# Back transform, join and first MLP steps of a long-convolution and MLP kernel: reordered hand-over between two stages

## The chip, the cores and the metric

The kernel runs on one core of a Trainium2 chip. The metric is the device time of one launch in microseconds; lower is better. A core has TensorE (PE in the rows, with PEld for its weight loads), VectorE (DVE), ScalarE (ACT), GpSimd (POOL) and SyncE (SP), which here only issues DMAs. ScalarE issues DMAs too.

## The reference

A long convolution by FFT, gated by its input, and then an MLP on all tokens (B = 2, S = 12480, D = 128, d_ff = 2048):

```python
h_filt = (np.maximum(pos_emb @ w1, 0.0) @ w2) * np.exp(-0.01 * pos)[:, None]
u = x * v
y = irfft(rfft(u, 2*S) * rfft(h_filt, 2*S), 2*S)[:, :S, :]   # along the sequence
a = (x * y).reshape(B * S, D)
h = a @ w_in
return np.maximum(0.01 * h, h) @ w_out
```

## The kernel before

The transform of length 98 x 128 is split into 98-point and 128-point parts that are matmuls with constant matrices. The program has three stretches:

- **First forward part of batch 0 and of the filter** (up to about 180 us of the span), bound by DMA.
- **The head's second stretch** (about 180 to 350 us), the loop `for i, c in enumerate(ORD)` over 25 chunks of four columns (`KC = 4`): forward 128-point transform (`fwd`), product with the filter's spectrum (`product`, multiplications and one addition on VectorE, the subtraction on GpSimd except in the last two rounds), back transform (`back_halves`, one round late), evacuation from PSUM (`evac`, both copies on ScalarE), store to the DRAM scratch `scr2`. The order ORD ends with chunks 10 and 11. The last two chunks also go straight from SBUF into the first tile's input `cin[0]` (`last_c`, eight small DMAs in all), so that the first tile need not wait for the scratch. Beside that, `weights()` (the generator `wprep`) splits the float64 MLP weights into two float32r parts; its last two operations make `wc_h` (ScalarE) and `wc_l` (VectorE).
- **The MLP** over 50 blocks of at most 512 tokens (block 0 has 390), each of 16 steps: `m1(k, f)` is three matmuls into `mh` (w_in_h by zh, w_in_h by zl, w_in_l by zh), ScalarE and VectorE make the two parts rh and rl of the activation, and three steps later `m2` adds three matmuls into `acc`.

A **tile t** is one pair of the 64 output pairs per batch. Its input `cin` is read from `scr2` (`upper_c`: five DMAs of the upper rows; `rows_c`: two of the lower rows), and `gt`, `xm` by `load_gx`. `join_hi` (two additions) and `join_lo` (six: two into `cq`, four into `cp`) put the halves together; `front` runs the last transform (16 matmul records into `yp`), multiplies by x (`zt`), transposes (`zp`), copies to `zf` (three ScalarE copies) and splits into zh (ScalarE) and zl. For tile 0 joins run on VectorE, for tiles 1 and 2 on GpSimd; tiles 0 and 1 share the one buffer of `cp`.

**Batch 1** is convolved by the generator `conv1`, whose pieces are spread between other work. Its first part has 16 groups of two halves; a half has four pieces: a pause, then eight matmuls and a ScalarE copy of the second PSUM tile, then VectorE's addition, then VectorE's subtraction (`add_sub`). The function `late()` stores the group before (two DMAs). `ahead(n)` runs n halves. Six halves and one piece (`AHEAD = 25`) run before the MLP's loop: two before the chunk loop, two between the loop and the last back transform, one after it, and one inside the first tile's front. The rest is paced from step 14 of the MLP on, so that the first part is done at step 120 whatever AHEAD is. `mult_a(c)` is GpSimd's product x*v for group c.

Each engine takes its instructions in program order (`manual_schedule`); GpSimd, having little before it, runs far ahead. SyncE takes nearly all loads and stores in program order and waits in order, so a load that waits for a store holds what stands behind it. Steps such as `turn_at`, `ends` and `at(i, what, t)` say at which MLP step a tile is loaded, joined, and put through its two halves of `front`: tile 1 at steps 2 and 5, tile 2 at 9 and 12, and `mult_a(3)` at 6.

## Time and profile before

| | |
|---|---|
| median of 3 runs | 1708.83 us (1698.93, 1708.83, 1709.12) |
| the profiled execution, its own time | 1702.05 us |
| its span, first to last instruction | 1700.3 us |
| granted TensorE clock, mean over the span | 0.980 |
| busy share of the span | TensorE 96%, VectorE 70%, ScalarE 59%, GpSimd 49% |

A time of the trace is counted from the span's start. A row of the timeline gives start, duration, engine, line of the kernel, operation, output and inputs, and how many instructions were merged; the bracket is the idle time of the engine before it and what ended it. Matmul records overlap, because matmuls are pipelined: the distance between two starts tells more than a duration. SPq and ACTq are the instructions that issue DMAs. A row of the windows gives the stretch, its length, each engine's busy time with its instructions, the granted TensorE clock as a share of full speed, the DMA engines' busy share and GB/s.

### The profile page before, as it was taken

The numbers are of one execution on the slowest core, as the hardware profiler recorded it, in microseconds if no ns is written. First come the engines' busy times: TensorE is split into PE (matmuls) and PEld (weight loads), VectorE is DVE, ScalarE is ACT, GpSimd is POOL, SyncE is SP. The second block draws the span as 40 slices with busy tenths as digits, with TensorE's granted clock in tenths as the row PEclk, the third lists the DMA queues.
The fourth block names the chain that finished last, engine by engine and source line by source line (L and its number), as shares of the span: only waits on it lengthen the run. The fifth ranks groups of instructions, "written<-read, shape, count | busy, mean of one in ns | idle before, by whom it ended". The sixth has DMA issues, their size and how long they took to land.

```text
span 1700.3 us, 27409 instructions
## 1 busy us (share of the span) xinstructions
PE 1635.3 (96%) x9173; PEld 1324.8 (78%) x9173; DVE 1183.0 (70%) x1774; ACT 1007.3 (59%) x2058; POOL 826.9 (49%) x810
## 2 busy tenths in 40 slices
PE   6788899889999999999999999999999999999998
PEld 5687456478888888888888888878888888887888
DVE  3566688855775565656666764787887877878765
ACT  1232355435664467677667766666766676666666
POOL 3454112244744266767666773644554544446410
PEclk9789899989999999999999999999999999999999
DMA  9898999965766466656556541321212212111100
GB/s 231 239 286 246 298 329 333 303 191 169 215 172 196 125 177 191 183 156 189 161 156 180 157 134 41 121 80 55 60 51 68 75 53 80 55 60 53 57 10 20
DMA packets 166423, 253.32 MB, mean 149 GB/s; under 512 B 14366, under 2 KB 119090, under 8 KB 163210
## 3 DMA queue, kind: packets, MB, share of 16 engines
q1 hardware_dynamic: 146650, 226.39, 45.9%
q10 hardware_dynamic: 19632, 25.18, 4.3%
q8 instruction: 73, 1.20, 0.3%
q14 instruction: 68, 0.56, 0.1%
HBM read 168.00 MB, written 83.43 MB: 148 GB/s over the span
## 4 chain that ended last, share of the span: by engine, by line
PE 79%; DVE 9%; DMA 7%; issue 2%; SPq 2%; ACT 1%; POOL 0%; ACTq 0%; DVEq 0%; POOLq 0%
PE mh L920 10%; PE acc L956 10%; PE acc L957 10%; PE mh L922 10%; PE acc L955 10%; PE mh L921 10%; PE cv L137 4%; PE yp L879 4%; PE cv L413 3%; PE a L375 2%; DVE rl L940 2%; PE op L979 2%; PE zp L898 1%; DMA scr<-o 1%; DMA xt<-in_x_dram 1%
## 5 line engine op out<-in xcount | busy, mean ns | idle before, releaser
L940 DVE TENSOR_TENSOR rl<-r,rh 128x512 fp32r<-128x512 f32 (+2 forms) x464 | 392.1, 863 | 96.1 <-ACT rh L939 87.5
L935 ACT ACTIVATE r<-mh 128x512 f32<-128x512 f32 (+2 forms) x464 | 270.9, 584 | 198.9 <-PE mh L922 180.1
L927 DVE SCALAR_TENSOR_TENSOR rl<-mh,rh 128x512 fp32r<-128x512 f32 (+1 forms) x336 | 227.7, 683 | 226.5 <-ACT rh L926 223.7
L920 PE MATMUL mh<-zh,w_in_h 128*128 128x512 f32 (+3 forms) x800 | 326.9, 409 | 1.3 <-ACT zh L911 1.3
L956 PE MATMUL acc<-rl,w_out_h 128*128 128x512 f32 (+3 forms) x800 | 309.8, 387 | 1.6 <-DVE rl L940 1.1
L955 PE MATMUL acc<-rh,w_out_h 128*128 128x512 f32 (+3 forms) x800 | 310.3, 388 | 0.0
L922 PE MATMUL mh<-zh,w_in_l 128*128 128x512 f32 (+3 forms) x800 | 310.2, 388 | 0.0
L957 PE MATMUL acc<-rh,w_out_l 128*128 128x512 f32 (+3 forms) x800 | 309.9, 387 | 0.0
L921 PE MATMUL mh<-zl,w_in_h 128*128 128x512 f32 (+3 forms) x800 | 309.6, 387 | 0.0
L926 ACT ACTIVATE rh<-mh 128x512 fp32r<-128x512 f32 (+1 forms) x336 | 199.5, 595 | 161.9 <-PE mh L922 153.8
L912 POOL TENSOR_TENSOR zl<-zf,zh 128x390 fp32r<-128x390 f32 (+24 forms) x110 | 69.0, 640 | 398.6 <-ACT zh L911 386.6
L645 POOL TENSOR_TENSOR cp<-cq,cp 98x256 f32<-98x256 f32 x252 | 223.7, 888 | 28.1 <-DVE cp L633 9.7
L937 DVE CAST rh<-r 128x512 fp32r<-128x512 f32 (+2 forms) x232 | 146.9, 633 | 55.9 <-ACT r L935 54.8
L956 PEld LDWEIGHTS acc<-rl,w_out_h 128*128 128x128 f32 x800 | 150.3, 188 | 39.2 <-DVE rl L940 7.8
L922 PEld LDWEIGHTS mh<-zh,w_in_l 128*128 128x128 f32 x800 | 150.8, 188 | 32.2
L920 PEld LDWEIGHTS mh<-zh,w_in_h 128*128 128x128 f32 x800 | 151.0, 189 | 31.3 <-issue 4.1
L957 PEld LDWEIGHTS acc<-rh,w_out_l 128*128 128x128 f32 x800 | 150.3, 188 | 30.6
L955 PEld LDWEIGHTS acc<-rh,w_out_h 128*128 128x128 f32 x800 | 150.4, 188 | 30.2
L921 PEld LDWEIGHTS mh<-zl,w_in_h 128*128 128x128 f32 x800 | 151.4, 189 | 24.4 <-DVE zl L912 0.3
L939 ACT CAST rh<-r 128x512 fp32r<-128x512 f32 (+2 forms) x232 | 140.6, 606 | 7.4
L642 POOL TENSOR_TENSOR cq<-cin 98x256 f32<-98x256 f32 x126 | 121.7, 966 | 2.4 <-DMA cin<-scr 2.4
L633 POOL TENSOR_TENSOR cp<-cin 98x256 f32<-98x256 f32 x78 | 75.6, 986 | 63.0 <-DMA cin<-scr 37.9
(155 smaller groups left out, 2396.3 us busy)
## 6 DMA issues: line engine op xcount, KB each, us to landing
cin<-scr SPq DMA_DIRECT2D x318, 98.0 KB
hd<-hspec SPq DMA_DIRECT2D x48, 512.0 KB
scr<-o SPq DMA_DIRECT2D x32, 588.0 KB
bin<-scr SPq DMA_DIRECT2D x23, 768.0 KB
scr<-ct SPq DMA_DIRECT2D x25, 512.0 KB
scr1b<-o SPq DMA_DIRECT2D x32, 392.0 KB
hspec<-hs ACTq DMA_DIRECT2D x48, 256.0 KB
xm<-in_x_dram SPq DMA_DIRECT2D x128, 96.0 KB
```

What stands on the lines that cost most here:

```text
L645: eng.tensor_tensor(out=cp[:, p, w], in0=cq[:, p], in1=cp[:, p, 1], op=op)
L920: nc.tensor.matmul(hp, w_in_h[:, fs], zh, start=True, stop=False)
L921: nc.tensor.matmul(hp, w_in_h[:, fs], zl, start=False, stop=False)
L922: nc.tensor.matmul(hp, w_in_l[:, fs], zh, start=False, stop=True)
L926: nc.scalar.activation(out=rh, in_=hp, func=AF.Relu)
L927: nc.vector.scalar_tensor_tensor(out=rl, in0=hp, scalar=0.0, in1=rh, op0=ALU.max, op1=ALU.subtract)
L935: nc.scalar.activation(out=r, in_=hp, func=AF.Lrelu, alpha=0.01)
L937: nc.vector.tensor_copy(rh, r)
L940: nc.vector.tensor_tensor(out=rl, in0=r, in1=rh, op=ALU.subtract)
L955: nc.tensor.matmul(ap, w_out_h[:, f, :], rh, start=(f == 0 and not sums(k)), stop=False)
L956: nc.tensor.matmul(ap, w_out_h[:, f, :], rl, start=False, stop=False)
L957: nc.tensor.matmul(ap, w_out_l[:, f, :], rh, start=False, stop=(f == NF - 1))
```

## The change

It moves work around the hand-over from the chunk loop to the MLP:

- In the last round, `product`'s subtraction runs on GpSimd again; `load_gx(1)` goes ahead of tile 0's `rows_c`, and the five loads `upper_c(1)` of tile 1 follow it, inside the loop.
- After the loop one half of `conv1` (in place of two) stands before the last back transform. `mult_a(2)` stands before it as well. The last evacuation copies one PSUM tile on ScalarE and one on VectorE. Of the last four small DMAs three go through SyncE and one through ScalarE.
- Then come `join_hi(0)`, the lower rows of tile 1, and two halves of `conv1` whose pieces leave PSUM by two ScalarE copies each and are added and subtracted by GpSimd (`add_sub_aside`). The store of group 1 is held back until tile 2's loads are issued. `AHEAD` is 21.
- `front0` replaces `front(0)`: the last transform and the product with x run in two steps, and zh and zl are made straight from PSUM (three ScalarE casts, three VectorE subtractions). The very first `m1` takes zl last.
- Tile 1 gets a buffer of its own for `cp`; its `join_hi` runs on GpSimd right after `front0`, its `join_lo` on VectorE in steps 2 to 4. Its front stands at steps 5 and 8, tile 2's at 10 and 13, the join of tile 2 at 4 as before, `mult_a(3)` at 9.

```diff
@@ -106,6 +106,16 @@
         nc.vector.tensor_tensor(out=dst0, in0=view(a0), in1=view(a1s[:, :n]), op=ALU.add)
         yield
         nc.vector.tensor_tensor(out=dst1, in0=view(a0), in1=view(a1s[:, :n]), op=ALU.subtract)
+
+    def add_sub_aside(a0, a1, dst0, dst1, view, t):
+
+        for i, a in enumerate((a0, a1)):
+            nc.scalar.copy(t[:a.shape[0], i], a)
+        yield
+        for dst, op in ((dst0, ALU.add), (dst1, ALU.subtract)):
+            nc.gpsimd.tensor_tensor(out=dst, in0=view(t[:a0.shape[0], 0]), in1=view(t[:a0.shape[0], 1]), op=op)
+            if op == ALU.add:
+                yield
 
     def run(g):
         for _ in g:
@@ -399,7 +409,10 @@
                 if PRE <= c < N1 - 1 and c + 1 not in got:
                     fetch_a(c + 1)
                 if late:
-                    late()
+                    if "held" in psc:
+                        psc["held"].append(late)
+                    else:
+                        late()
                 o = sc.tile([128, 2048], F32, tag="s4", name="o1")[:NA, :4 * MC1 * D].rearrange(
                     "a (r m s d) -> a r m s d", r=2, s=2, d=D)
                 for h in range(MC1 // 2):
@@ -414,8 +427,12 @@
                                                  ft[:, 2 * h + j, p, NA * ri:NA * ri + NA], uh[:, p, 2 * h + j, :],
                                                  start=True, stop=True)
                     ms = slice(2 * h, 2 * h + 2)
-                    yield from add_sub(sc, a[0], a[1], o[:, :, ms, 0, :], o[:, :, ms, 1, :],
-                                       lambda t: t.rearrange("a (r m d) -> a r m d", r=2, d=D), 1)
+                    outs = (o[:, :, ms, 0, :], o[:, :, ms, 1, :],
+                            lambda t: t.rearrange("a (r m d) -> a r m d", r=2, d=D))
+                    if "aside" in psc:
+                        yield from add_sub_aside(a[0], a[1], *outs, psc.pop("aside")())
+                    else:
+                        yield from add_sub(sc, a[0], a[1], *outs, 1)
                     yield
                     if h == 0 and PRE <= c < N1 - 1:
                         mult_a(c + 1)
@@ -529,8 +546,8 @@
 
         conv = conv1()
         pieces = N1 * (MC1 // 2) * 4 + WAIT + 3 + 15 * NCH - 3
-        A0, A1, A2, A3, A4, A5 = 2, 2, 0, 1, 1, 0
-        AHEAD = 1 + 4 * (A0 + A1 + A2 + A3 + A4 + A5)
+        A0 = 2
+        AHEAD = 1 + 4 * (A0 + 3)
 
         mlp = ctx.enter_context(tc.tile_pool(name="mlp", bufs=2, reuse_waits="tile"))
         class Ring:
@@ -610,9 +627,9 @@
 
         def last_c(ct, k0, n, engs):
 
-            for r in range(2):
-                for m in range(2):
-                    engs[m].dma_start(out=cin[0][KH * r + k0:KH * r + k0 + n, 0, m],
+            for m in range(2):
+                for r in range(2):
+                    engs[2 * m + r].dma_start(out=cin[0][KH * r + k0:KH * r + k0 + n, 0, m],
                                       in_=ct[HB * r + m:HB * r + m + 1, :n])
 
         def load_tile(t):
@@ -623,7 +640,10 @@
 
             ci_t = cin.pop(t)
             eng = nc.vector if t == 0 or 8 <= t < NT else nc.gpsimd
-            if t in second:
+            if t == 1:
+                cp = psc["pool"].tile([128, 2048], F32, tag="hd", name="cp2", bufs=2)[:NA, :1024].rearrange(
+                    "k (p w m d) -> k p w m d", p=2, w=2, m=2)
+            elif t in second:
                 cp = aside("cp2")[:NA].rearrange(
                     "k (p w m d) -> k p w m d", p=2, w=2, m=2)
             else:
@@ -637,7 +657,7 @@
 
             ci_t, cp = cps[t]
             cq = mlp.tile([NA, 2, 2, D], F32, tag="cq", name="cq", bufs=1)
-            eng = nc.gpsimd if t else nc.vector
+            eng = nc.gpsimd if t > 1 else nc.vector
             for p, op in ((0, ALU.add), (1, ALU.subtract)):
                 eng.tensor_tensor(out=cq[:, p], in0=ci_t[:, 0, :, 0, :], in1=ci_t[:, 0, :, 1, :], op=op)
                 yield
@@ -754,9 +774,14 @@
                 ct = sbb.tile([128, KC, 2, D], F32, tag="ct", name="ct", bufs=2)
                 k0, n = chunk(c)
                 end = c == ORD[-1]
-                run(back_evac(dps.pop(c), ct, n))
+                dp = dps.pop(c)
+                if end:
+                    for s, copy in ((0, nc.scalar.copy), (1, nc.vector.tensor_copy)):
+                        copy(ct[:, :n, s, :], dp[s][:, :n * D].rearrange("p (k d) -> p k d", d=D))
+                else:
+                    run(back_evac(dp, ct, n))
                 if c in ORD[-2:]:
-                    last_c(ct, k0, n, (nc.sync, nc.scalar if end else nc.sync))
+                    last_c(ct, k0, n, [nc.sync] * 3 + [nc.scalar if end else nc.sync])
                 store_back(0, c, ct, nc.sync if end else nc.scalar)
 
             eh, dps = {}, {}
@@ -772,8 +797,9 @@
                 if i == NCH - 2:
                     load_gx(0)
                 if i == NCH - 1:
+                    load_gx(1)
                     rows_c(0, 0, 0, (MID - 2) * KC)
-                    load_gx(1)
+                    run(upper_c(1))
                 if i in FETCH:
                     fetch_a(1 + FETCH.index(i))
                 if i == NCH - 2:
@@ -804,7 +830,7 @@
                     next(wprep, None)
                 pins[c] = sbb.tile([128, 2, 512], F32, tag="pin", name="pin", bufs=2)
                 ab = [sbb.tile([128, 2, 512], F32, tag=g, name=g) for g in ("ta", "tb")]
-                product(ab, up, hs, n * D, pins[c], nc.vector if i >= NCH - 2 else nc.gpsimd)
+                product(ab, up, hs, n * D, pins[c], nc.vector if i == NCH - 2 else nc.gpsimd)
                 if i >= 1:
                     b4 = ORD[i - 1]
                     dps[b4] = two("d")
@@ -818,18 +844,18 @@
                     f()
                 late.clear()
 
-            for _ in range(4 * A1 - 1):
-                next(conv)
+            ahead(1)
+            run(wprep)
+            mult_a(2)
             dps[ORD[-1]] = two("d")
             back_halves(dps[ORD[-1]], pins.pop(ORD[-1]), ORD[-1])
             evac(ORD[-1])
-            next(conv)
-            load_c(1)
-            mult_a(2)
-            ahead(A2)
-            run(wprep)
             run(join_hi(0))
-            ahead(A3)
+            rows_c(1, 0, 0, KH)
+            psc["held"] = []
+            for g in ("ta", "tb"):
+                psc["aside"] = lambda g=g: sbb.tile([128, 2, 512], F32, tag=g, name=g)
+                ahead(1)
 
 
         sm = ctx.enter_context(tc.tile_pool(name="sm", bufs=2, reuse_waits="tile"))
@@ -912,14 +938,44 @@
                 (nc.gpsimd if t else nc.vector).tensor_tensor(out=zl, in0=zf[:, c:c + n], in1=zh, op=ALU.subtract)
             yield
 
+        def front0():
+
+            g, xt = ld.pop(0)
+            cp = cps.pop(0)[1]
+            yp = ps.tile([128, 4, D], F32, tag="io", name="yp")
+            zp = ps.tile([128, WIDE], F32, tag="acc1", name="zp", bufs=1).rearrange("a (q d) -> a q d", d=128)
+            zt = sm.tile([128, 856], F32, tag="zt", name="zt", bufs=1)[:, :4 * D].rearrange("a (q d) -> a q d", d=D)
+            z[0] = [sm.tile([128, WIDE], F32R, tag=i, name=i, bufs=ZB) for i in ("zh", "zl")]
+            for p in range(2):
+                for q in (2 * p, 2 * p + 1):
+                    for w in range(2):
+                        nc.tensor.matmul(yp[64 * w:64 * w + 64, q, :], g[:NA, NA * q + w:NA * q + w + 127:2],
+                                         cp[:, p, w, q % 2, :], start=True, stop=True)
+                nc.vector.tensor_tensor(out=zt[:GAP, 2 * p:2 * p + 2], in0=yp[:GAP, 2 * p:2 * p + 2],
+                                        in1=xt[:GAP, p], op=ALU.mult)
+            for q in range(4):
+                nc.tensor.transpose(zp[:, q, :GAP], zt[:GAP, q, :], ident[:GAP, :GAP])
+
+            def parts(t):
+                yield (t[:, 2 * NA - 2:TOK].rearrange("d (m i w) -> d m w i", m=2, w=2),
+                       zp[:, 0:2].rearrange("d m (w i) -> d m w i", w=2)[:, :, :, :KH])
+                for w in range(2):
+                    yield (t[:, :2 * NA - 2].rearrange("d (m a) -> d m a", m=2)[:, :, w::2],
+                           zp[:, 2:4, 64 * w:64 * w + KH - w])
+            zh, zl = z[0]
+            for o, i in parts(zh):
+                nc.scalar.copy(o, i)
+            for (o, i), (h, _) in zip(parts(zl), parts(zh)):
+                nc.vector.tensor_tensor(out=o, in0=i, in1=h, op=ALU.subtract)
+
         def m1(k, f):
             w = widths[k]
             zh, zl = (i[:, :w] for i in z[k])
             hp = ps.tile([128, WIDE], F32, tag="mh", name="mh", bufs=3)[:, :w]
             fs = slice(f * 128, f * 128 + 128)
-            nc.tensor.matmul(hp, w_in_h[:, fs], zh, start=True, stop=False)
-            nc.tensor.matmul(hp, w_in_h[:, fs], zl, start=False, stop=False)
-            nc.tensor.matmul(hp, w_in_l[:, fs], zh, start=False, stop=True)
+            for i, (u, m) in enumerate(((w_in_h, zh), (w_in_l, zh), (w_in_h, zl)) if k == f == 0 else
+                                       ((w_in_h, zh), (w_in_h, zl), (w_in_l, zh))):
+                nc.tensor.matmul(hp, u[:, fs], m, start=(i == 0), stop=(i == 2))
             rh = sm.tile([128, WIDE], F32R, tag="rh", name="rh", bufs=DEEP + 2)[:, :w]
             rl = sm.tile([128, WIDE], F32R, tag="rl", name="rl", bufs=DEEP + 2)[:, :w]
             if sums(k):
@@ -1018,6 +1074,8 @@
                 q = turn_at[t - 2]
                 gets[t] = ((q if t > 4 else ends[t - 2]) + 1 if t - 2 not in leads | second else
                            q - 5 if t in leads else q - 1)
+        turn_at[1], turn_at[2] = 5, 10
+        ends[1], ends[2] = 8, 13
         for t in range(1, total):
             g, p = turn_at[t], turn_at.get(t - 1, 0)
             if t in leads:
@@ -1031,8 +1089,11 @@
                 lo = max(g - 9, p + 1, gets[t] + 5)
                 for n in range(8):
                     at(lo + (g - 1 - lo) * n // 8, "sum", t)
+            elif t == 1:
+                for n in range(6):
+                    at(2 + n // 2, "sum", t)
             elif t not in second:
-                at(g - 5, "join", t)
+                at(4 if t == 2 else g - 5, "join", t)
             if t not in second:
                 at(g, "front", t)
                 if t in leads:
@@ -1047,7 +1108,7 @@
             elif t == 2:
                 at(0, "load", t)
 
-        at(6, "mult", 3)
+        at(9, "mult", 3)
 
         def do(what, t, i):
             if what == "mult":
@@ -1077,17 +1138,15 @@
 
         SLOTS = ends[NT] - 14
         done = AHEAD
-        frt = front(0)
-        next(conv)
         run(join_lo(0))
-        next(frt)
+        front0()
+        joins[1] = join(1)
+        for _ in range(2):
+            next(joins[1])
         load_tile(2)
+        for f in psc.pop("held"):
+            f()
         fetch_a(3)
-        for _ in range(4 * A4 - 1):
-            next(conv)
-        run(frt)
-        for _ in range(4 * A5):
-            next(conv)
         STAGE1 = N1 * (MC1 // 2) * 4
         FROM, TILL = 14, 120
 
```

## Rows read from the trace of the kernel before

**Rows 1.** The page, part 1: busy time, share of the span, instructions.

```profile
PE 1635.3 (96%) x9173; PEld 1324.8 (78%) x9173; DVE 1183.0 (70%) x1774; ACT 1007.3 (59%) x2058; POOL 826.9 (49%) x810
```

**Rows 2.** Windows: us, busy (instructions) of PE, PEld, DVE, ACT, POOL; PE clock.

```profile
355.00:360.00 5.00, 3.48 (x11) 2.83 (x12) 2.25 (x5) 1.63 (x5) 3.06 (x5) 0.50 0.47 153
...
370.00:380.00 10.00, 10.00 (x69) 9.54 (x68) 5.11 (x10) 5.15 (x15) 4.79 (x5) 1.00 0.78 224
```

**Rows 3.** Timeline of PE, 340 to 365 us.

```profile
342.55 1.99 PE L151 MATMUL dp<-pin,mi 64*128 64x512 f32 x8
...
349.89 2.66 PE L413 MATMUL cv<-xv,ft 98*98 98x128 f32 x16 [3.43 <-DVE o L108]
352.49 1.98 PE L879 MATMUL yp<-cp,gt 98*64 98x128 f32 x16
355.26 1.01 PE L898 MATMUL zp<-ident,zt 113*128 113x113 f32 x4 [0.79 <-DVE zt L889]
357.53 0.69 PE L920 MATMUL mh<-zh,w_in_h 128*128 128x390 f32 x1 [1.26 <-ACT zh L911]
...
361.03 0.74 PE L879 MATMUL yp<-cp,gt 98*64 98x128 f32 x8
...
363.43 0.45 PE L920 MATMUL mh<-zh,w_in_h 128*128 128x390 f32 x1
```

**Rows 4.** The chain that ended last, 360 to 390 us: start, us, what.

```profile
372.13 1.03 PE yp L879 x16
...
376.54 0.39 PE zp L898 x4
...
381.41 1.75 PE cv L413 x16
```

**Rows 5.** Timeline of DVE, 320 to 365 us.

```profile
324.04 0.74 DVE L132 TENSOR_TENSOR pin<-ta,tb 128x512 f32<-128x512 f32 x1
...
325.09 2.19 DVE L692 TENSOR_TENSOR w_in_l<-wi,w_in_h 128x256 fp32r<-128x256 f32 x1 [0.31 <-ACT w_in_h L690]
...
333.35 2.45 DVE L132 TENSOR_TENSOR pin<-ta,tb 128x512 f32<-128x512 f32 x1
...
340.18 0.69 DVE L132 TENSOR_TENSOR pin<-ta,tb 128x512 f32<-128x512 f32 x1
340.82 0.29 DVE L720 TENSOR_TENSOR wc_l<-wcs,wc_h 128x128 fp32r<-128x128 f32 x1
...
349.07 0.68 DVE L108 TENSOR_TENSOR o<-hp,a1s 98x512 f32<-98x512 f32 x1
350.35 0.42 DVE L642 TENSOR_TENSOR cq<-cin 98x256 f32<-98x256 f32 x1 [0.60 <-issue]
```

**Rows 6.** Timeline of POOL, 315 to 345 us.

```profile
322.95 1.28 POOL L132 TENSOR_TENSOR pin<-ta,tb 128x512 f32<-128x512 f32 x1 [4.79 <-DVE tb L131]
324.19 2.81 POOL L233 TENSOR_TENSOR xv<-xv,xv 98x1024 f32<-98x1024 f32 x1
332.91 2.35 POOL L233 TENSOR_TENSOR xv<-xv,xv 98x1024 f32<-98x1024 f32 x1 [5.90 <-DMA xv<-in_v_dram]
```

**Rows 7.** Timeline of ACT, 325 to 365 us.

```profile
344.56 1.07 ACT L209 COPY ct<-dp 128x512 f32<-128x512 f32 x2 [1.06 <-PE dp L151]
345.67 2.07 ACTq L615 DMA_DIRECT2D cin<-ct x2
...
356.57 0.35 ACT L903 COPY zf<-zp 128x196 f32<-128x196 f32 x1
356.96 0.52 ACT L911 CAST zh<-zf 128x390 fp32r<-128x390 f32 x1
```

**Rows 8.** Line 615, its DMA issues on SP: min/median/max ns.

```profile
L615 SPq DMA_DIRECT2D cin<-ct x6: 572/572/789, 340.1 to 346.3; - x6
```

**Rows 9.** Timeline of DVE, 869 to 875 us.

```profile
870.24 3.47 DVE L633 TENSOR_TENSOR cp<-cin 98x256 f32<-98x256 f32 x1
```

**Rows 10.** Timeline of POOL, 869 to 875 us.

```profile
870.89 2.54 POOL L525 TENSOR_TENSOR pl<-usp,ph 128x512 fp32r<-128x512 f32 x2
```

## The prediction

> **What bounds the kernel.** I read the page first: TensorE is busy 96% of the span, VectorE 70% [rows 1]. So the end is set by TensorE's work plus the places where it stands still or runs at the low clock. The windows say where these are: from 370 us on it is busy for the whole stretch at full clock, between 355 and 360 us it is busy 3.48 of 5 us, and the granted clock is 0.50, the 1.2 GHz level [rows 2]. The timeline of TensorE then shows the hand-over step by step [rows 3]: last back transform at 342.55, one half of conv1 behind it until 346.5, nothing for 3.43 us, another half at 349.89, tile 0's last transform `yp` at 352.49, its transposes at 355.26, the first MLP matmul at 357.53, tile 1's transform at 361.03 with a second part late, and a steady stream only from 363.43. In a stretch where TensorE is the bound, a half taken out of the head is paid again later, at full clock: 1.75 us by the chain [rows 4]. So my sum has three terms: when the first MLP matmul starts (before: 357.53), the half that goes into the MLP (+1.75), and what is lost between the first MLP matmul and the steady stream. That last is now 363.43 - 357.53 = 5.90 us for nine matmuls and one `yp`. The nine ran at the low clock in 361.03 - 357.53 = 3.50 us, so about 1.75 us at full clock, and `yp` takes 1.03 there [rows 4]; 3.1 us are lost.
>
> **What sets 357.53.** VectorE's join of tile 0 starts at 350.35, and VectorE had just ended the half's subtraction at 349.75 [rows 5]. The data came earlier: the eight small DMAs are all issued by 347.74 [rows 7]. The join is six operations of 0.43 us, 2.6 in all, so it ends at 352.95; from there to the first matmul pass 4.6 us.
>
> **The change, part by part.** *Last transform sooner.* The second of two halves stood between the product and the back transform `dp`. The product's last addition ended at 340.87 [rows 5]; with the 0.69 us subtraction on GpSimd (1.28 there [rows 6]) it ends near 340.2. The product's six operations take about 0.65 each and the subtraction is the third, so GpSimd starts it at 338.3 and ends at 339.6, beside VectorE's last two multiplications. TensorE reaches `dp` when one half is done: 342.55 less a half of about 1.8 is 340.75. So `dp` ends at 342.7 instead of 344.54. *Evacuation on two engines.* ScalarE took 1.07 for both copies [rows 7]; side by side they take about 0.7 (bounds: a VectorE operation on 512 columns takes 0.68 [rows 5]). Chunk 11 would be in SBUF at 343.4 instead of 345.63.
>
> *What speaks against it* is VectorE's order. `wc_l` and the half's addition and subtraction (2 x 0.68) stand ahead of its copy. In the trace of before `w_in_l`, the same kind of operation, took 2.19 us, and the product's addition 2.45, both beside a running `mult_a` on GpSimd, and both ended just after it [rows 5, 6]; an addition alone takes 0.69. The changed program puts `mult_a(2)` exactly there: from 339.6 GpSimd goes on with 2.35 to 2.81 us of `mult_a(2)` [rows 6], to about 342.5. `wc_l`, ready at 340.8, then ends at 342.7 instead of 341.1, the two operations of the half at 344.0, the copy at 344.6. Bounds for the copy's end: 343.4 (not blocked) and 344.6; I take 344.6, because the rows show just this pair. The gain to here is 1.0 us, not 2.2.
>
> *Small DMAs.* SyncE's cost 0.57 each [rows 8], ScalarE's two took 2.07 [rows 7]. Three on SyncE end 1.75 us after the copy, 346.35; before, the last issue ended 2.1 after it. The rows bound the landing between 0 and 2.6 us behind the last issue (347.74 to 350.35); I take 0.8, near a single small issue. Data at 347.1. The five loads of `upper_c(1)` on SyncE, about 3 us at 0.57 each, fit between tile 0's `rows_c` and chunk 10's small DMAs; if they don't, chunk 10 comes later but still before chunk 11, so nothing.
>
> *Join of tile 0.* VectorE no longer has the half's two operations ahead of it, so it could start at 347.1 instead of 350.35. But the halves' four operations now run on GpSimd, 1.28 each (a 512-column operation [rows 6]), from SBUF. GpSimd can begin when ScalarE, behind its small DMA (0.6 to 1.4), has made two copies (1.15): 344.6 + 1.8 to 2.6 = 346.4 to 347.2. That is a tie with the join. If VectorE is first, its six operations follow each other without a gap and GpSimd waits: join done at 349.7. If GpSimd is first, VectorE waits for one operation (rest at most 1.28): 351.0. If it waits for all four, and for tile 1's `join_hi` (2 x 0.73) behind them, until 353: 355.6. Later in the trace one addition of the join took 3.47 us, where one of that size takes 0.42 [rows 5], while GpSimd ran an operation that ended about 870.9 and then two of 1.27 each, so several operations can go by [rows 9, 10]. *A rule on this.* The Trainium skill, page SBUF — State Buffer, section Who interferes with whom, says that a VectorE operation with two SBUF inputs and a GpSimd operation that reads SBUF exclude each other for the length of one instruction. The trace agrees on the exclusion (2.19 and 2.45 us [rows 5, 6]) and shows a wait over more than one instruction (3.47 us [rows 9, 10]). By the rule alone the join would be done by 351.0 at the latest. I take 351.0, the middle, from the rows.
>
> *`front0`.* The first half of `yp` runs under the second half of the join. What is left after it: half of `yp` (0.5 at full clock, 1.0 at the low one [rows 3, 4]), half of the product (0.35), transposes 0.39 to 1.01 [rows 3, 4], casts in three pieces, about 0.35 + 2 x 0.25 where before three copies and a cast of 0.52 stood [rows 7], and some 0.7 of hand-overs: 3.3 us at the low clock, against 4.6. First MLP matmul: 351.0 + 3.3 = 354.3, which is 3.2 sooner.
>
> *After it.* `join_hi(1)` is done long before, so the 0.64 us of waiting for GpSimd in tile 1's `yp` and the halved clock under it could go. But tile 1's `join_lo` puts 6 x 0.43 us on VectorE in the first six steps, beside six `rl` (0.68 x 390/512 = 0.52 each) and zl (0.6): 6.3 us, against 30 matmuls of 0.19, 5.8 us, at full clock. VectorE starts one matmul and one ScalarE operation behind TensorE, so it would be the later of the two by about 1.4 us at full clock, and by none at the low one, where TensorE itself loses up to 3.1. I take 2.1, between these, in place of 3.1. *At nothing* I count `upper_c(1)`, `load_gx(1)`, the held store (group 1 is read only after step 120) and the moved `mult_a(3)`: the steady stream covers them [rows 2]. If the store of chunk 11 held `rows_c(1)` and tile 2 behind it on SyncE, tile 2's `yp` at step 10 would be late; it has some 7 steps of six matmuls, 1.1 us each, in hand. The front of tile 2 at 13, one step later, leaves block 1 one step less for zl: at most 0.4 us.
>
> **The sum.** -3.2 (start) + 1.75 (the half) - 1.0 (after it) = -2.45, with +0.4 at worst for block 1. Against the profiled execution's own 1702.05 that is 1699.6.
>
> **Rivals.** *GpSimd keeps VectorE out* until its four operations and `join_hi(1)` are done: join done at 355.6, first matmul at 358.9, +1.4 + 1.75 - 1.0 = +2.1, 1704.2: slower than before. It decides from the point where GpSimd's operations begin before the join's first. For it the 3.47 us [rows 9, 10]; against it, that at 324.2 an addition of VectorE's went in between two operations of GpSimd that followed each other: it took only 0.74 [rows 5], and the `mult_a` behind it 2.81 instead of 2.35 [rows 6]. *VectorE becomes the bound of the first six steps*, with the join late by one or two operations: no gain after the start, start at 355.5, -2.0 + 1.75 + 0 = 1701.8: no change. *The pause of TensorE gets so short that the clock does not fall*: `yp`, transposes and nine matmuls at full clock give another 3 us, with VectorE first: start at 352, 1694 to 1696. Against it: the low stretch of before came after a pause of 3.43 us and one half [rows 2, 3], and a pause from 346.5 to the first `yp` near 349.7 is about as long.
>
> **How the numbers follow.** Forecast 0.45, its own range -5 to -1, so 1697 to 1701; GpSimd keeps VectorE out 0.25; VectorE bound 0.2; no low clock 0.1. About 1% is what a measurement of this kernel can tell from no change: the runs shown lie 10 us apart, and the profiled one is 6.8 under their median. No case reaches 17 us. I leave 0.04 and 0.03 for a difference beyond 1% that no row prices, and 0.93 within it. The profiled time and the three runs have a mean of 1704.7; I take the forecast from there, 1704.7 - 2.45 = 1702. The range goes from the fastest run less 5, 1694, to the slowest with the slow rival's 2.1, 1711.
>
> **What would show it.** Right: `dp` at about 340.8; `wc_l` near 2 us long, beside `mult_a`; the last copy at 344.6; a join operation of 1 us or more; first MLP matmul at 354; the stream from 360. Wrong: `wc_l` at 0.3, a join without gaps or one that ends after 355, low clock gone, or TensorE waiting after step 16.

## The result and the profile after

| | before | after |
|---|---|---|
| median | 1704.50 us (6 runs, 1698.93 to 1709.12) | 1718.49 us (6 runs, 1716.83 to 1723.16) |
| profiled execution, its own time | 1702.05 us | 1722.75 us |
| its span | 1700.3 us | 1721.0 us |

The ratio is 1.0087, with an interval of 1.0069 to 1.0105: the change makes the kernel 14.0 us slower, within 1% but clearly outside the predicted 1694 to 1711.

The page of the changed kernel (busy time, share of the span, instructions; it answers to [rows 1]):

```profile
PE 1646.9 (96%) x9173; PEld 1323.8 (77%) x9173; DVE 1194.5 (69%) x1779; ACT 1007.8 (59%) x2058; POOL 828.5 (48%) x809
```

TensorE executes the same 9173 matmuls as before, and is busy 1646.9 us with them instead of 1635.3. That is 11.6 us of busy time, beside 14.0 in the medians. A hand-over that goes wrong adds idle time first, and busy time only in the few matmuls that it leaves at the low clock. So this one line already points away from the hand-over as the main thing.

The windows around the hand-over (columns as in [rows 2]):

```profile
355.00:360.00 5.00, 1.88 (x10) 1.11 (x12) 4.77 (x5) 0.00 (x0) 4.22 (x4) 0.50 0.24 72
360.00:365.00 5.00, 4.30 (x18) 3.08 (x19) 1.25 (x5) 1.11 (x4) 1.46 (x2) 0.50 0.56 179
370.00:380.00 10.00, 10.00 (x79) 9.12 (x78) 5.66 (x12) 4.51 (x11) 7.65 (x8) 1.00 0.65 176
```

The picture is that of before: a stretch with a waiting TensorE at the 1.2 GHz level (0.50), then a full one at 1.00. It lies later, though, and in part that has nothing to do with the change. The last round's forward transform starts at 339.01 us here; in the ten experiments below it starts at 330.2 to 339.6 in the three with the old order, at 332.4 to 337.1 in the seven with the new one, and in the trace of before at 332.86. So the traces are compared from that point, called **up** from here on: from up to the end of the span it is 1367.4 us before and 1382.0 after, 14.5 more, close to the 14.0 between the medians.

The timeline of TensorE (columns as in [rows 3]), with the hand-over first and three places of the MLP behind it:

```profile
339.01 1.94 PE L133 MATMUL up<-bin,mb 128*64 128x512 f32 x8 [1.92 <-DVE ta L141]
...
345.36 1.99 PE L161 MATMUL dp<-pin,mi 64*128 64x512 f32 x8
...
349.11 1.91 PE L426 MATMUL hp<-xv,ft 98*98 98x128 f32 x16
355.06 0.66 PE L952 MATMUL yp<-cp,gt 98*64 98x128 f32 x2 [4.05 <-issue]
356.42 1.11 PE L952 MATMUL yp<-cp,gt 98*64 98x128 f32 x6 [0.70 <-DVE cp L665]
359.89 1.12 PE L952 MATMUL yp<-cp,gt 98*64 98x128 f32 x8 [2.36 <-DVE zt L954]
360.94 1.24 PE L957 MATMUL zp<-ident,zt 113*128 113x113 f32 x4
362.88 0.69 PE L978 MATMUL mh<-zh,w_in_h 128*128 128x390 f32 x1 [0.70 <-ACT zh L967]
...
367.35 0.45 PE L1008 MATMUL acc<-zl,wc_h 128*128 128x390 f32 x1
...
1233.72 0.40 PE L978 MATMUL mh<-zh,w_in_h 128*128 128x512 f32 x1
...
1411.08 0.40 PE L978 MATMUL mh<-zh,w_in_h 128*128 128x512 f32 x1
...
1412.47 0.40 PE L978 MATMUL mh<-zh,w_in_h 128*128 128x512 f32 x1
...
1697.91 0.32 PE L978 MATMUL mh<-zh,w_in_h 128*128 128x352 f32 x1
```

The hand-over: the back transform at up + 6.35 (before + 9.68), a pause of 4.05 us ahead of `yp`, then two further waits of 0.70 and 2.36 us inside it, first MLP matmul at up + 23.88 (before + 24.67). So by these two traces the hand-over is 0.8 us shorter, not longer. The loss is behind it. The first matmuls of block 30 (1233.72) and of block 49 (1697.91) are 464.19 us apart. In the timeline of TensorE before, the same two matmuls are 459.47 apart:

```profile
1217.76 0.39 PE L920 MATMUL mh<-zh,w_in_h 128*128 128x512 f32 x1
...
1677.23 0.32 PE L920 MATMUL mh<-zh,w_in_h 128*128 128x352 f32 x1
```

Nothing in these 19 blocks was edited. From block 4 to block 48 a block of after is 0.26 us longer on average, and the loss is spread: the largest single one is 1.4, in block 10. Six 512-column matmuls take 1412.47 - 1411.08 = 1.39 us after. The mean distance of two starts between 1150 and 1650 us (distances of 300 ns and more left out) is 232.7 to 233.8 ns by kind of matmul, and 227.8 to 230.7 before, while the distances of the transposes, which read other tiles, are unchanged (97 ns).

VectorE, GpSimd, ScalarE around the hand-over (these answer to [rows 5 to 7]). First VectorE:

```profile
344.34 0.77 DVE L142 TENSOR_TENSOR pin<-ta,tb 128x512 f32<-128x512 f32 x1
345.38 2.09 DVE L740 TENSOR_TENSOR wc_l<-wcs,wc_h 128x128 fp32r<-128x128 f32 x1 [0.27 <-ACT wc_h L739]
...
348.58 0.67 DVE L780 COPY ct<-dp 128x512 f32<-128x512 f32 x1
...
352.26 1.30 DVE L662 TENSOR_TENSOR cq<-cin 98x256 f32<-98x256 f32 x1 [2.34 <-DMA cin<-ct]
353.60 2.77 DVE L665 TENSOR_TENSOR cp<-cq,cp 98x256 f32<-98x256 f32 x2
356.29 1.49 DVE L662 TENSOR_TENSOR cq<-cin 98x256 f32<-98x256 f32 x1
357.81 1.69 DVE L665 TENSOR_TENSOR cp<-cq,cp 98x256 f32<-98x256 f32 x2
```

Then GpSimd:

```profile
344.50 2.81 POOL L243 TENSOR_TENSOR xv<-xv,xv 98x1024 f32<-98x1024 f32 x1
352.00 2.68 POOL L116 TENSOR_TENSOR o<-ta 98x512 f32<-98x512 f32 x2 [4.69 <-ACT ta L113]
354.65 2.85 POOL L116 TENSOR_TENSOR o<-tb 98x512 f32<-98x512 f32 x2
357.46 1.76 POOL L653 TENSOR_TENSOR cp<-cin 98x256 f32<-98x256 f32 x2
```

And ScalarE:

```profile
349.33 1.42 ACTq L632 DMA_DIRECT2D cin<-ct  x1
350.85 1.07 ACT L113 COPY ta<-up 98x512 f32<-98x512 f32 x2 [2.89 <-PE hp L426]
```

The join of tile 0 takes from 352.26 to 359.50, 7.24 us for six operations that took 2.60 before. GpSimd's four additions and subtractions begin 0.26 us ahead of it, and they and tile 1's `join_hi` behind them (L653) run beside it nearly to its end. One by one, the six operations of the join end 0.28 or 0.29 us after six operations of GpSimd (the first at 353.56 after 353.28, the last at 359.50 after 359.22). `wc_l` takes 2.09 us beside `mult_a(2)`.

### The profile page after: what moved, and what is told of

It reads as the page before. It is cut to its first block, busy times and chain, and to the rows that moved or that the text cites. A ratio compares the mean times of both kernels' runs of the same rounds, so it can differ in the third digit from the quotient of the medians.

```text
span 1721.0 us, 27430 instructions
## 1 busy us (share of the span) xinstructions
PE 1646.9 (96%) x9173; PEld 1323.8 (77%) x9173; DVE 1194.5 (69%) x1779; ACT 1007.8 (59%) x2058; POOL 828.5 (48%) x809
## 4 chain that ended last, share of the span: by engine, by line
PE 80%; DMA 9%; DVE 5%; issue 2%; SPq 1%; ACT 1%; ACTq 0%; POOL 0%; DVEq 0%; POOLq 0%
PE mh L978 30%; PE acc L1012 10%; PE acc L1013 10%; PE acc L1011 10%; PE cv L147 4%; PE yp L905 4%; PE cv L426 3%; DMA scr<-ct 2%; PE a L385 2%; DMA xt<-in_x_dram 2%; PE op L1035 2%; PE zp L924 1%; DMA scr<-o 1%; PE up L133 1%; DVE rl L996 1%
## 5 line engine op out<-in xcount | busy, mean ns | idle before, releaser
L996 DVE TENSOR_TENSOR rl<-r,rh 128x512 fp32r<-128x512 f32 (+2 forms) x464 | 398.3, 875 | 105.3 <-ACT rh L995 97.1
L142 POOL TENSOR_TENSOR pin<-ta,tb 128x512 f32<-128x512 f32 (+1 forms) x24 | 30.1, 1253 | 144.6 <-DVE tb L141 144.6
```

Of the source, the lines that this page charges most:

```text
L996: nc.vector.tensor_tensor(out=rl, in0=r, in1=rh, op=ALU.subtract)
```

## The experiments

**What differs in the steady part.** The same instructions are slower, so what can differ is where their operands lie. The built programs give each tile an address. `zh`, `zl`, `rh` and `rl`, the moving operands of the MLP's matmuls, lie in the pool `sm` behind `zt` (3424 bytes per partition) and `zf` (1560). In the kernel before, `zt` and `zf` are allocated first and `zh` starts at byte 149696, an odd multiple of 64, as do the others. `front0` makes zh and zl straight from PSUM, so it allocates `zh` before any `zf`: `zh` starts at 148128, and all four start 32 bytes past a multiple of 64. The PSUM tiles also got other banks (`mh` 2 to 4 in place of 3 to 5, `acc` and `cv` others too). Two theories, then: SBUF addresses or PSUM banks. The next four kernels are compared with 15 runs of the kernel before (median 1703.65).

**e1_after_aligned** is the changed kernel with a wider `zt`, in both places, so that the four tiles start at multiples of 64 again:

```diff
-                zt = sm.tile([128, 856], F32, tag="zt", name="zt", bufs=1)
+                zt = sm.tile([128, 864], F32, tag="zt", name="zt", bufs=1)
```

> The changed kernel with one number altered: the tile zt is 864 instead of 856 columns wide (its first 512 are used). That puts zh, zl, rh and rl, which the MLP's matmuls read as moving operands, at SBUF addresses that are multiples of 64 bytes, where the kernel before has them; in the changed kernel they lie 32 bytes off. Nothing else of the program changes; PSUM banks stay as in the changed kernel. Theory address: the 13 us that the MLP lost come from there. From one matmul to the next of 512 columns it takes 226 to 232 ns again (changed kernel: 231 to 235), and the time falls by 12 to 14 us to about 1705. Theory banks (mh, acc and cv lie in other PSUM banks than before): 1718, no change. Theory order (the work that moved into the MLP, or late tiles, costs the 13 us): 1718, no change.

**e2_before_shifted** is the kernel before with the same line. There it moves the four tiles 32 bytes off.

> The kernel before with the same one number altered, 864 instead of 856 columns for zt: there it moves zh, zl, rh and rl from multiples of 64 bytes to 32 bytes off. Nothing of the hand-over changes. Theory address: slower by 12 to 14 us, about 1717 to 1719, with the matmuls' distance at 231 to 235 ns all through the MLP and the hand-over as before (first MLP matmul 24.7 us after the start of chunk 11's forward transform). Theory banks and theory order: 1704.5, as before.

**e3_before_128** is the kernel before with 520 in place of 856: the four start at multiples of 128.

> The kernel before with zt 520 columns wide, which puts zh, zl, rh and rl at multiples of 128 bytes (before: multiples of 64 but odd ones). If 64 is all that counts: 1704.5, distances 226 to 232 ns. If 128 counts too: faster by some us, distances near 225 ns throughout. Theory banks and theory order: 1704.5.

**e4_before_offsets** is e3 with the four operands at different starts within wider tiles: `zh` 16 bytes past a multiple of 128, `zl` 48, `rh` 4, `rl` 0.

```diff
-                    z[k] = [sm.tile([128, WIDE], F32R, tag=g, name=g, bufs=ZB) for g in ("zh", "zl")]
+                    z[k] = [sm.tile([128, WIDE + 32], F32R, tag=g, name=g, bufs=ZB)[:, s:s + WIDE]
+                            for g, s in (("zh", 4), ("zl", 12))]
...
-            rh = sm.tile([128, WIDE], F32R, tag="rh", name="rh", bufs=DEEP + 2)[:, :w]
+            rh = sm.tile([128, WIDE + 32], F32R, tag="rh", name="rh", bufs=DEEP + 2)[:, 1:1 + w]
```

> The kernel before with wider tiles of which a part is used, so that each kind of moving operand starts at another offset from a multiple of 128 bytes: zh 16 bytes, zl 48, rh 4, rl 0. The distances behind matmuls with each are read apart. Theory address, by the start's offset in 64 bytes: 226 to 232 ns behind rl, 231 to 236 behind zl, zh and rh; the time some 8 to 14 us above the kernel before. If only an offset of 32 and more costs, zh and rh stay at 226 to 232. Theories banks and order: all as before.

| | start of the moving tiles | median us (runs) | ratio to before | mean distance of 512-column matmuls by kind, ns (those under 300) |
|---|---|---|---|---|
| before | 64 past a multiple of 128 | 1703.65 (15) | | 227.8 to 230.7 |
| after | 32 past a multiple of 64 | 1718.49 (6) | 1.0087 [1.0069, 1.0105], to 1704.50 (6) | 232.7 to 233.8 |
| e1 | 64 past a multiple of 128 | 1707.96 (10) | 1.0026 [1.0014, 1.0038] | 228.0 to 230.6 |
| e2 | 32 past a multiple of 64 | 1716.02 (4) | 1.0071 [1.0052, 1.0090] | 232.8 to 234.2 |
| e3 | multiple of 128 | 1699.25 (6) | 0.9969 [0.9952, 0.9986] | 227.5 to 228.6 |
| e4 | 16, 48, 4, 0 past one | 1712.62 (1) | | 229.9 to 235.4 |

The timelines of TensorE show it in the first matmuls of blocks 30 and 49. e1, 459.28 us apart:

```profile
1222.86 0.39 PE L978 MATMUL mh<-zh,w_in_h 128*128 128x512 f32 x1
...
1682.14 0.32 PE L978 MATMUL mh<-zh,w_in_h 128*128 128x352 f32 x1
```

e2, 464.68:

```profile
1224.69 0.39 PE L920 MATMUL mh<-zh,w_in_h 128*128 128x512 f32 x1
...
1689.37 0.33 PE L920 MATMUL mh<-zh,w_in_h 128*128 128x352 f32 x1
```

e3, 456.62, with six matmuls in 1.36 us in between:

```profile
1219.12 0.39 PE L920 MATMUL mh<-zh,w_in_h 128*128 128x512 f32 x1
...
1411.47 0.39 PE L920 MATMUL mh<-zh,w_in_h 128*128 128x512 f32 x1
...
1412.83 0.39 PE L920 MATMUL mh<-zh,w_in_h 128*128 128x512 f32 x1
...
1675.74 0.32 PE L920 MATMUL mh<-zh,w_in_h 128*128 128x352 f32 x1
```

What follows: one number in one allocation takes 10.5 us from the changed kernel (1718.49 to 1707.96) and puts 12.4 on the kernel before (1703.65 to 1716.02). TensorE's busy time follows: 1633.5 us in e1 and 1645.9 in e2, against 1635.3 before and 1646.9 after. e1 keeps the new PSUM banks and e2 the old ones, so the banks are out. The addresses are what slowed the steady part. It is TensorE's reading that suffers and not the writing of these tiles: VectorE's subtraction into `rl` takes 0.90 us on average both before and after, ScalarE's cast into `rh` 0.62. e4 moves nothing but these operands within their tiles, and its one run is 13.4 us above e3. It doesn't give a rule, though: behind `zh`, 16 bytes off, the next matmul comes after 229.9 to 230.5 ns, no slower than before but 2 to 3 ns slower than in e3, from which e4 is made; behind `zl` (48) after 233.5, behind `rh` (4) after 234.8 to 235.4, and behind `rl`, which is aligned but always has `rh` as its neighbour, after 232.3.

**What is left: 4.3 us.** e1 has the addresses' class of before and the change's hand-over, and is still 4.3 us slower (interval 2.4 to 6.5). So what is left of the change doesn't win the predicted 2.45, it loses. Theories: GpSimd's halves beside the join; `wc_l` behind `mult_a(2)`; the half that went into the MLP. The next four kernels are compared with 31 runs of the kernel before (median 1704.20); the first three start from e1.

**e5_no_gpsimd_halves**: the two halves use VectorE's `add_sub` again.

```diff
-            for g in ("ta", "tb"):
-                psc["aside"] = lambda g=g: sbb.tile([128, 2, 512], F32, tag=g, name=g)
-                ahead(1)
+            ahead(2)
```

> e1_after_aligned with the two halves of conv1 behind the last back transform done as before (ScalarE copies one PSUM tile, VectorE adds and subtracts) instead of by two copies and GpSimd. GpSimd is then silent while VectorE joins tile 0. Theory port: the six operations of the join, which took 7.2 us from 352.26 in the changed kernel, take 2.6 again; but four operations of 0.68 stand ahead of them, so the join ends some 2 us sooner and the time falls by about 2 us. Theory late data (the join waits for its small DMAs, not for GpSimd): the join is stretched as before and the time stays at 1708 or rises by the 2.7 us of VectorE's work.

Measured: 1702.92 us (10 runs), ratio 0.9989 [0.9976, 1.0002], 5.0 less than e1. In its timeline of VectorE the join runs without gaps, 2.58 us, while `wc_l` still takes 1.79:

```profile
342.09 1.79 DVE L740 TENSOR_TENSOR wc_l<-wcs,wc_h 128x128 fp32r<-128x128 f32 x1 [0.56 <-ACT wc_h L739]
...
351.17 0.41 DVE L662 TENSOR_TENSOR cq<-cin 98x256 f32<-98x256 f32 x1
351.62 0.88 DVE L665 TENSOR_TENSOR cp<-cq,cp 98x256 f32<-98x256 f32 x2
```

Putting those halves on GpSimd was worse than leaving them on VectorE, although VectorE then starts the join 1.4 us later (table below).

**e6_wcl_later**: `wc_h` and `wc_l` move behind the last copies.

```diff
-                for _ in range(2):
+                for _ in range(2 if i < NCH - 1 else 0):
                     next(wprep, None)
...
-            run(wprep)
             mult_a(2)
...
             run(join_hi(0))
+            run(wprep)
```

> e1_after_aligned with the last split of the weights (wc_h, wc_l) taken out of VectorE's queue ahead of the half and the last copy, and put behind tile 0's two upper joins; it is needed only in step 3. Theory port: the 2.09 us that wc_l took beside mult_a(2) are gone (0.3 where it stands now), the last copy ends 1.2 to 1.8 us sooner against the back transform, and the small DMAs with it. The time falls by about 1 us, or by nothing where GpSimd's four operations then meet the join all the same. Theory late data: as theory port for the copy, and the whole 1.2 to 1.8 us come through.

Measured: 1707.63 us (10 runs), ratio 1.0020 [1.0008, 1.0032], the same as e1. In its timeline of VectorE `wc_l` takes 0.29, and the join is still stretched, to 5.62:

```profile
343.52 0.29 DVE L740 TENSOR_TENSOR wc_l<-wcs,wc_h 128x128 fp32r<-128x128 f32 x1 [1.29 <-ACT wc_h L739]
346.98 1.58 DVE L662 TENSOR_TENSOR cq<-cin 98x256 f32<-98x256 f32 x1 [3.17 <-DMA cin<-ct]
348.59 2.23 DVE L665 TENSOR_TENSOR cp<-cq,cp 98x256 f32<-98x256 f32 x2
```

The copies are 1.1 us sooner, and GpSimd still begins its halves ahead of the join. Of the gain 0.7 us are left at the first MLP matmul (23.54 from up against 24.22), too little for the runs to tell.

**e7_both**: e6, with the first of the two halves by VectorE's `add_sub`, and the second copied by ScalarE and added and subtracted by VectorE in steps 7 and 8 of the MLP. GpSimd has nothing beside the join.

> e1_after_aligned with wc_l later as in e6, the first of the two halves behind the back transform added and subtracted by VectorE in the time in which it waits for the small DMAs, and the second copied out of PSUM by ScalarE as in the changed kernel but added and subtracted by VectorE at steps 7 and 8 of the MLP. GpSimd has nothing to do with two SBUF inputs until tile 1's upper join. Theory port: the join takes 2.6 us plus what tile 1's upper join on GpSimd still takes from it (up to 1.5), the first MLP matmul comes 4 to 5 us sooner against chunk 11's forward transform (24.2 in e1), the time falls to about 1703. Theory late data: no more than 1 us.

Measured: 1703.03 us (10 runs), ratio 0.9991 [0.9977, 1.0006]. The join takes 2.60, the first MLP matmul comes at up + 20.86, 3.4 us sooner than in e1, where 4 to 5 were expected; of that e5 had 2.5 already, and the runs don't tell e5 and e7 apart.

**e8_both_128**: e7 with `zt` 528 wide, so that the four tiles start at multiples of 128.

> e7 with zt 528 columns wide, so that zh, zl, rh and rl lie at multiples of 128 bytes, as in e3. Theory address: 4 us less than e7, by the 4.4 us that e3 was under the kernel before: about 1699, the same as e3 or a little less.

Measured: 1699.14 us (10 runs), ratio 0.9966 [0.9951, 0.9981]. That is e3's ratio: at equal addresses the mended hand-over, over 4 us sooner at the first MLP matmul, equals the old one. So those 4.3 us (19.61 against 23.91 in the table below) are paid again in the MLP, by the start of block 10 (325.34 us from up, 325.13 in e3), and the half's 1.75 is not enough to account for them.

**Where they are paid.** Block by block, e1, e5 and e7 lose 1.2 to 1.3 us to before in block 2 and again in block 3, and about nothing in the others behind block 0. The waits of TensorE between 420 and 520 us (the line that waits, what it waits for, us in total, times, longest) say for what. Before:

```profile
PE cv L413 <- DVE o L108: 0.6, 1, 0.6
```

e1:

```profile
PE cv L426 <- DVE o L108: 2.1, 3, 1.0
```

The transforms of `conv1` wait for VectorE to empty PSUM. With `AHEAD` 21, 128 - 21 = 107 pieces are spread over the 106 steps from 14 to 120; before it was 103. That doesn't put two pieces into one step: by the kernel's formula, 21 + 107 * (i - 14) // 106, every step from 15 to 119 gets exactly one. What changes is the steps on which a half's matmuls stand. In the traces of e1 and e8 they are at 15, 19, 23 and so on to 119; before, with three steps left empty, at 16, 20 and so on to 48, then at 53 and so on. The three waits are at steps 35, 63 and 71, the one of before is at 69. The longest can be followed in e8. On TensorE:

```profile
475.30 0.90 PE L429 MATMUL cv<-xv,ft 98*98 98x128 f32 x6 [1.03 <-DVE o L108]
```

On VectorE, where the subtraction of the half before stands behind an `rl` of 2.76 us:

```profile
471.88 2.76 DVE L1000 TENSOR_TENSOR rl<-r,rh 128x512 fp32r<-128x512 f32 x1
474.57 0.68 DVE L108 TENSOR_TENSOR o<-cv,a1s 98x512 f32<-98x512 f32 x1
```

On GpSimd, beside that `rl` (at 469.49, with GpSimd standing still, an `rl` takes 0.69):

```profile
471.53 2.57 POOL L246 TENSOR_TENSOR xv<-xv,xv 98x1024 f32<-98x1024 f32 x1
```

Two more kernels, made from e8, are compared with 11 runs of the kernel before (median 1703.58):

**e9_pace** begins the pacing four steps earlier, so 107 pieces have 110 steps:

```diff
-        FROM, TILL = 14, 120
+        FROM, TILL = 10, 120
```

> e8 with the pacing of conv1 in the MLP started at step 10 instead of 14. The changed kernel leaves 107 pieces for 106 steps (before: 103), so now and then two pieces fall into one step and a half's matmuls come three steps after the last, when VectorE has not yet emptied its PSUM tile: in e1, e5, e7 TensorE waited there three times for 2.1 us (before: once, 0.6), in blocks 2 and 3. With 107 pieces over 110 steps that is gone. Theory pace: 1.5 us of waits less, blocks 1 to 10 take 281.2 instead of 282.7 us, the time falls by about 1.5 us to 1697.5. If the waits had another cause: no change, 1699.

Measured: 1693.22 us (6 runs), ratio 0.9941 [0.9926, 0.9957]. The waits of TensorE in the same stretch:

```profile
PE cv L429 <- DVE o L108: 0.7, 1, 0.7
```

Against e8, blocks 2 and 3 are 1.42 and 1.19 us shorter, 2.6 together, about what they had lost and more than the 1.5 expected. The expectation's reason doesn't hold, though: in e8 no half comes three steps after the last, all are four apart. In e9 the halves stand at 12, 16 and so on to 44, then 49, 53 and so on, nearly the steps of before, and again only the wait at step 69 is left. The slow `rl` is there in e9 too, at step 61, with no half behind it that TensorE waits for. The medians differ by 5.9, against different runs of the kernel before; the ratios' intervals just overlap, so the trace's 2.6 is the part with a cause.

**e10_half_in_gap** goes the other way from e8: a third half in the head, in TensorE's pause before `yp`, by ScalarE and GpSimd, with its last piece left to the MLP, so that 104 pieces are left:

```diff
-        AHEAD = 1 + 4 * (A0 + 3)
+        AHEAD = 4 * (A0 + 4)
...
             ahead(1)
+            psc["aside"] = lambda: sbb.tile([128, 2, 512], F32, tag="ta", name="ta")
+            for _ in range(3):
+                next(conv)
```

> e8 with a third half of conv1 put back into the head, behind the other two, where TensorE stands still before tile 0's last transform; ScalarE copies it out of PSUM, GpSimd adds and subtracts. The half no longer has to be paid in the MLP. Theory port, as the runs so far show it: GpSimd reaches its addition when VectorE's join is running without a gap and has to wait, so the join stays at 2.6 us; blocks 1 to 10 fall by 1.75 (the half) and 1.5 (no two pieces in a step), the first MLP matmul comes at most 1 us later: 2 to 3 us less than e8, 1696 to 1697. If GpSimd comes first, the join is stretched by 1.3 to 5 us and nothing is won.

Measured: 1694.24 us (6 runs), ratio 0.9941 [0.9919, 0.9963]. From up to block 10 it is 321.07 us, 4.3 less than e8: the half (block 0 is 1.7 shorter) and the pacing (blocks 1 to 9, 3.5 shorter), less 1.0 for a later start (in this trace the forward transform itself took 3.62 us instead of 1.94, with the granted clock at 0.57 from 334 to 338 us). The expected 2.6 us of join didn't come: GpSimd's input is ready late, its pair starts when four of the join's operations are done, and the join's last operation waits for it, so the join takes 3.53. VectorE's timeline there, the join's last three operations:

```profile
349.75 0.42 DVE L669 TENSOR_TENSOR cq<-cin 98x256 f32<-98x256 f32 x1
350.19 1.83 DVE L672 TENSOR_TENSOR cp<-cq,cp 98x256 f32<-98x256 f32 x2
```

And GpSimd's, which holds the last two back to 1.83 from 0.89:

```profile
350.45 2.74 POOL L118 TENSOR_TENSOR o<-ta 98x512 f32<-98x512 f32 x2 [6.32 <-ACT ta L115]
```

The whole table, worked out from the ten traces and the two first ones (us; starts and ends are counted from up, a block from its first matmul to that of the next):

| | `wc_l` took | last copy's end | join's start | join took | first MLP matmul | block 0 | blocks 1 to 9 | blocks 30 to 48 |
|---|---|---|---|---|---|---|---|---|
| before | 0.29 | 12.77 | 17.48 | 2.60 | 24.67 | 22.49 | 280.97 | 459.47 |
| after | 2.09 | 10.25 | 13.26 | 7.24 | 23.88 | 23.05 | 285.78 | 464.19 |
| e1 | 1.95 | 10.26 | 14.30 | 6.54 | 24.22 | 23.73 | 283.67 | 459.27 |
| e2 | 0.29 | 11.19 | 15.88 | 2.60 | 23.41 | 24.64 | 283.87 | 464.68 |
| e3 | 0.28 | 11.19 | 15.88 | 2.60 | 23.91 | 22.13 | 279.09 | 456.62 |
| e4 | 0.29 | 11.19 | 15.90 | 2.60 | 23.42 | 24.40 | 283.28 | 463.75 |
| e5 | 1.79 | 10.24 | 15.73 | 2.58 | 21.74 | 23.27 | 283.50 | 459.58 |
| e6 | 0.29 | 9.12 | 14.53 | 5.62 | 23.54 | 23.11 | 283.52 | 459.39 |
| e7 | 0.29 | 9.12 | 14.88 | 2.60 | 20.86 | 23.72 | 283.47 | 459.57 |
| e8 | 0.29 | 9.12 | 13.63 | 2.60 | 19.61 | 22.99 | 282.74 | 456.70 |
| e9 | 0.29 | 9.12 | 13.92 | 2.60 | 19.94 | 23.46 | 279.88 | 456.63 |
| e10 | 0.29 | 10.81 | 14.36 | 3.53 | 20.58 | 21.30 | 279.19 | 456.68 |

e2, e3 and e4 have the hand-over of before, and start the MLP 0.8 to 1.3 us sooner than the trace of before does: there the product's addition was held for 2.45 us by a `mult_a` [rows 5, 6], which these three traces don't show. So the one trace on which the prediction was built had a hand-over about 1 us longer than usual.

## Why the prediction was wrong

**The time.** 1702 was forecast and 1718.49 came, 7.5 above the range. The change of 0.87% lies within the 1% that had 0.93, but the forecast's sign was a gain.

**The step that failed first is one that the sum doesn't have.** The prediction priced what the new instructions cost and what moved. It did not ask where the tiles lie. It said of the steady stream only that it covers the edits counted "at nothing"; that stream itself became slower, by 10.5 us in the changed kernel (against e1) and 12.4 in the kernel before (e2). The cause is the line of `front0` that allocates `zh` and `zl` ahead of `zf`, which the diff shows. No row of before could have priced it, because all its moving tiles lay alike. But the question could have been asked: each new or reordered tile in a pool moves those behind it, and a range that took this in as an unknown cost would have been wider on both sides, as e2 and e3 show for one and the same line.

**The hand-over, step by step** (times as distances from up, 332.86 before and 339.01 after).
- *Last transform sooner*: predicted at + 7.9, measured + 6.35. Right, and 1.5 us better: the product ended at + 6.10, where + 7.3 was counted from a trace in which a `mult_a` had held an addition shortly before (e2 to e4, with the old order, have + 6.75, the trace of before + 8.01).
- *`wc_l` beside `mult_a(2)`*: about 2 us predicted, 2.09 measured. Right, but worth less than thought: without it (e6) the time is the same.
- *Last copy*: predicted + 11.7, measured + 10.25.
- *The tie of join and GpSimd*: predicted as a tie, measured 0.26 us apart, GpSimd first. Here the second step failed. The middle value was one operation of GpSimd's, a join of 2.6 + 1.28. It took 7.24: each operation of VectorE's ran in turn with one of GpSimd's, past GpSimd's last of four and through `join_hi(1)`. The join's end came at + 20.5, where the forecast was + 18.1 and the rival "GpSimd keeps VectorE out" + 22.7. The rival's condition came true (GpSimd begins first) and its mechanism didn't: VectorE was not kept out until all was done, it got one operation in after each of GpSimd's, at a price between. e5 and e7 show it from the other side: without GpSimd's operations the join takes 2.58 and 2.60, and e5 is 5.0 us faster than e1 in the medians (2.25 from up to the end in the traces).
- *On the rule.* The Trainium skill, page SBUF — State Buffer, section Who interferes with whom, calls the shared port pair an exclusive lock, and has it that the order of issue decides who blocks. The trace agrees for each single operation (1.30 us for one of 0.42, with GpSimd's of 1.27 beside it). The prediction's "by 351.0 at the latest" does not follow from this: it counted one wait, and the wait comes again at every operation while both engines have work, 4.6 us in all here.
- *`front0`*: 3.3 us predicted from the join's end to the first matmul, 3.38 measured (359.50 to 362.88). Right.
- *First MLP matmul*: predicted + 21.4, measured + 23.88; a gain of 0.8 us, where 3.2 were counted. Against the usual hand-over of before (e2 to e4, + 23.4 to + 23.9) it is no gain at all.

**The half (+1.75)**: right. In e10, with the half back in the head, block 0 is 1.69 us shorter than in e8: e8 has 16 of `conv1`'s matmuls in block 0, e10 none, and blocks 1 to 7 have the same number in both.

**After it (-1.0)**: the size is about right. Thirteen matmuls run from 362.88 to 367.35 at the low clock, 4.47 us, where the later ones of the same size are 0.173 apart: 2.2 lost, 2.1 predicted. For equal work, thirty MLP matmuls and tile 1's transform, it is 8.70 us after (362.88 to 371.58), 9.27 in e1 and 9.78 before (357.53 to 367.31): -1.1 and -0.5. TensorE waits nowhere in this stretch, so the rival with VectorE as its bound is out.

**"Paced so that the first part is done at step 120 whatever AHEAD is"** was taken to cost nothing beside the half itself. This is the third step that failed: with four pieces more in the same 106 steps the halves move to other steps, and that costs 2.4 to 2.6 us in blocks 2 and 3; e9, which moves them back, regains it. (Of the 2.5 in e1, 1.5 are recorded as waits, and `conv1`'s matmuls in these blocks take 2.3 more in all.) The prediction had named "TensorE waiting after step 16" as a sign of being wrong. The waits are for VectorE, whose 70% of the span [rows 1] is a mean and doesn't show that it is late in single steps. Why VectorE is late at steps 35 and 71 stays open.

**The sum with the measured terms**, e1 against the trace of before: start -0.45, block 0 +1.24 (the half's 1.75 less the 0.5 after the start), blocks 1 to 9 +2.70 (mostly pacing), +3.5 up to block 10; behind it blocks 10 to 48 are 1.6 shorter (0.6 of it one longer block in the trace of before), so +1.8 from up to the end, against +4.3 [2.4, 6.5] by the runs. So the sum gives the sign, and 2.5 of the 4.3 have no place in it: these are two single executions, and that of before has the long hand-over. The addresses are 10.5 by the medians (after against e1), 12.7 by the two traces from up to the end.

**The low clock stayed**, as forecast: the granted clock is 0.50 from 355 to 365 us in the windows of after, and the rival that needed 1.00 there is out.

**A version that beats both.** Three things are mended in it: the tiles' addresses, GpSimd's halves and the pacing. e9 and e10 are 10.4 and 9.3 us faster than the kernel before; e3 shows that 4.4 us come from one number and need no change of the order at all. What is left for the mended order is about 5 us by the ratios (0.9941 against e3's 0.9969, with intervals that just overlap), and 3.4 and 4.2 us from up to the end in the traces (1355.8 and 1355.0 against 1359.3).

## What to carry to other kernels

When a diff allocates a tile in a new place or order, compare the start addresses of the operands that the bound engine streams before and after, because the cost falls on every instruction of the steady part and no timeline of the edited stretch shows it; TensorE's busy time at an unchanged count is the first line to look at. Do not give GpSimd two-input work beside a chain of VectorE operations on the critical path: count the chain as running in turn with it, not as one wait. And where work is taken out of one stage and put into a paced one, check on which steps the pieces land before and after, because the other engines are not equally free in each.

## What the runs showed of the hardware

- **The start of a matmul's moving operand in SBUF changes its rate.** With 512 float32r columns at full clock, the mean distance of two matmuls is 227.5 to 228.6 ns with tiles that start at multiples of 128 bytes (e3), 227.8 to 230.7 at odd multiples of 64 (before), and 232.8 to 234.2 at 32 past a multiple of 64 (e2): 1699.25, 1703.65 and 1716.02 us for one and the same kernel. Why it is so, and what single offsets of 4, 16 and 48 bytes do by themselves, stays open; in e4's one run 16 bytes cost 2 to 3 ns against e3, 4 and 48 bytes 6 to 8.
- The Trainium skill, page SBUF — State Buffer, section Operand start alignment, says that an operand has to start at a multiple of its element's size, and that this is about legality and not speed. All starts here are legal by it, and in these runs they differ in speed.
- **VectorE and GpSimd take turns**, one operation each, while both have two-input work in SBUF: six operations of VectorE's took 7.24 us instead of 2.60, each ending 0.28 or 0.29 us after one of GpSimd's, and GpSimd's pairs took 2.68 and 2.85. In the trace of before one operation of VectorE's waited for several [rows 9, 10]; what decides between the two was not tried.
- **A small DMA's issue took longer on ScalarE than on SyncE**: 1.42 us in the ScalarE row above (1.18 to 1.46 in the changed kernels' traces), where SyncE's seven of that line have a median of 0.572 us, as before [rows 8]. Of two such issues in a row on ScalarE in the trace of before, the first took 1.41 and the second 0.63.
